# Load order, state decay on ScalarE, early attention values, and down layers with the weight units outermost

## The chip, the core and the metric

The kernel runs on one core of one Trainium2 chip. The time is that of the device, in microseconds (us), from the launch on the core to its end. Three runs of the kernel before gave 545.58, 546.04 and 546.85, so its time is the median, 546.04 us. The engines are named as in the profile: PE is TensorE, PEld its weight loads, DVE VectorE, ACT ScalarE, POOL GpSimd, and SP the engine that issues every DMA here.

## The reference

Three layers follow one another. The first is attention with a decay per head (2 sequences, 8 heads, 768 positions, 64 wide); the second multiplies two projections; the third takes the largest of three.

```python
for b in range(nb):                       # blocks of 64 positions
    intra = einsum(einsum(qb, kb) * Dmask, vb)
    inter = einsum(qb * lam_pow, kv_state)
    out[:, :, sl] = intra + inter
    kv_state = lam_block * kv_state + einsum(kb * rev_pow, vb)
x = out as (1536 tokens, 512)
x = ((x @ w_a) * (x @ w_b)) @ w_out                     # inner width 1536
y = max(max(x @ w1, x @ w2), x @ w3) @ w_out2           # inner width 768
```

q, k, v are float32; the weights are float64.

## The kernel before

**Numbers.** A weight block comes in as raw 64-bit words (`wr`, two buffers). `converted` makes float32 of it with six passes: DVE L223, ACT L226, DVE L228, ACT L231, ACT L233, DVE L235. An ACT copy (L190) then makes the high part and a DVE or POOL subtraction (L187) the low part. Every product of two float32 matrices is three matmuls: high by high, high by low, low by high. The operands x and y are split in the same way.

**Stages.** In the order of time:
- Attention works in 12 chunks n of 128 positions, the two sequences in turn. `scores(n)` is 16 matmuls (L395) into two PSUM banks, `side(n)` scales q and k on POOL (L405, L408), `masked(n)` multiplies the scores by the decay table on DVE (L418, tile `am`), and `values(n)` has up to 48 matmuls: am by v (L434), the state `stt` by q (L439) and the new state (L446). ACT then copies the result out (`x`), and DVE adds the new state to the decayed one (L458 or L460) and decays it for the chunk after the next (L463). Chunk n+2 of the same sequence needs both.
- From n = 7 on, a quarter of the first layer's plain products (L552, tile `p`) follows each chunk; then come the other groups of that layer in seven products each (L534, `zu`, `bu`, `xu`).
- `down1` (L657, tile `yp`): three tiles of 512 tokens, each of 12 units of 128 inner columns, each unit 12 matmuls over four banks. The tile is the outer loop, so each unit of the weights is wanted by the first tile 12 matmuls after the last one.
- The second layer's groups (L534, `zv`, `bv`, `xv`), whose results are folded into `m`.
- `down2` (L685, tile `out`): 12 tiles of 128 rows, each of 6 units of 3 matmuls. The weights come in four blocks of 1.5 units.

**Order.** Every engine runs its instructions in program order. A small model of the engines' times (`Pace`) sets in which order the queued tasks (conversions, splits) are written on DVE, ACT and POOL among the fixed work; `open_to` says from which point on a conversion ("conv") or its split may be written. SP issues the loads in order and waits at each until its buffer is free, so that a load of `wr` which waits for a buffer holds all later loads back. `converted` asks for the raw block two further on (L229) as soon as it has read its own.

Of the kernel before, what the change touches and what calls it, by code (L numbers as in the profile page):

```python
# [13 lines left out]
ALU = mybir.AluOpType  # L14
# [148 lines left out]
def decay_attention_gated_mlps(ctx: ExitStack, tc: tile.TileContext, qkv: bass.AP, lam: bass.AP, wup: bass.AP, wdown: bass.AP, out: bass.AP):  # L163
# [48 lines left out]
    def converted(m, width, roomy=False):  # L212
# [65 lines left out]
    def down_block(m, i):  # L278
        roomy = 2 <= i < ND1 or i == ND1 + 3
        yield "gate", ("done", m - (2 if roomy else 1))  # L280
# [12 lines left out]
        tt(e, lo[:, s], t[:, 0:WB], rd(hi[:, s]), ALU.subtract)  # L293
        pace.open(("done", m))
        for k in range(3):
            if k // 2 <= i % 2 and (i // 2, k) not in dunit and (k == 0 or i % 2):
                dunit[i // 2, k] = hi[:, 512 * k:512 * k + 512], lo[:, 512 * k:512 * k + 512]

    def items_to(m):
        while state["item"] <= min(m, len(items) - 1):  # L300
            n = state["item"]
            kind, i = items[n]
            wtask[n] = pace.opens["done", n] = pace.add((up_pair if kind == "up" else down_block)(n, i), 1 if n > 1 else -1)
            state["item"] += 1
# [72 lines left out]
    def load(n, *which):  # L377
# [4 lines left out]
        for i in which:  # L382
            of, name = ((aq, "aq"), (av, "av"))[i]
            of[n] = slot(f"{name}{n}")
            nc.sync.dma_start(out=of[n][:, 0:1024], in_=qkv[b * NC + c, i])

# [35 lines left out]
    def values(n):  # L422
# [31 lines left out]
        if c < NC - 1:  # L454
# [19 lines left out]
    class Operands:  # L474
# [5 lines left out]
        def __init__(self, a, name, order=ORDER):  # L480
# [7 lines left out]
            for i, x in enumerate(order):  # L488
                t = self.tasks[x] = pace.add(self.make(i, x, "A21" in order), 0)
                for g in ("sum", "part"):  # L490
# [140 lines left out]

    gparts, gtasks = {}, {}

    def splits_to(n):
        while len(gtasks) < min(n, NTT * K1):
            i = len(gtasks)
            t, k = divmod(i, K1)
# [3 lines left out]
            gtasks[i] = pace.add(split_part(ga[k][:, 512 * t:512 * t + 512], h, l), 0), h, l  # L641

    def down1(at):
        n = NTT * K1
        for i in range(n):
            t, k = divmod(i, K1)
            at(t, k)
            splits_to(i + 3)
            if k == 0:
                ps = [bank(f"yp{t}{e}") for e in range(KD)]  # L650
            wh, wl = unit(0, k)
            task, gh, gl = gtasks[i]
            pace.need(task)
            for e in range(KD):
                cols = slice(128 * e, 128 * e + 128)
                for m, (w, g) in enumerate(((wh, gh), (wh, gl), (wl, gh))):
                    nc.tensor.matmul(ps[e], w[:, cols], g, start=k == 0 and m == 0, stop=k == K1 - 1 and m == 2)  # L657
                pace.pe(3 * MM5)
                if k == K1 - 1:
                    o = 512 * t  # L660
                    while o < 512 * t + 512:
                        q, r = divmod(o, J)
                        m = min(J - r, 512 * t + 512 - o)
                        j, b = divmod(q, 2)
                        if (j, b) not in ya:
                            ya[j, b] = slot(f"y{j}{b}").rearrange("p (a i) -> p a i", a=KD)
                        copy(ya[j, b][:, e, r:r + m], ps[e][:, o - 512 * t:o - 512 * t + m])
                        pace.run("ACT", m)
                        o += m

    def down2(i):
        j, b, r = i // 6, i // 3 % 2, i % 3
        o = tokens(j, b).start + 128 * r
        row = b * S + j * J + 128 * r
        last = i == NT // 128 - 1
        cols = 256 if last else 512
        ob = slot(f"ob{i}")
        for c in range(0, 512, cols):
            s = slice(c, c + cols)
            ps = bank(f"out{i}_{c}")[:, s]  # L680
            for k in range(K2):
                (ah, al), (wh, wl) = hs[k], unit(ND1, k)
                pace.need(htask[k, j])
                for n, (a, w) in enumerate(((ah, wh), (al, wh), (ah, wl))):
                    nc.tensor.matmul(ps, a[:, o:o + 128], w[:, s], start=k == 0 and n == 0, stop=k == K2 - 1 and n == 2)  # L685
                pace.pe(3 * MM5 * cols / 512)
            if last and c > 0:
                nc.vector.tensor_copy(ob[:, s], ps)  # L688
            else:
                copy(ob[:, s], ps)  # L690
                pace.run("ACT", cols)
            nc.sync.dma_start(out=out[row:row + 128, s], in_=ob[:, s])

    with tc.manual_schedule():
# [8 lines left out]
        ps = bank("warm_ps")  # L703
        for i in range(9):
            nc.tensor.matmul(ps, warm[:, 0:128], warm, start=True, stop=True)
        powers()
# [7 lines left out]
        pace.t["PE"] = 6.0  # L714
        for n in range(3):
            scores(n)
        pace.t["PE"] = 12.0
        for n in range(2):
# [49 lines left out]
        for n in range(len(order)):  # L768
            load(n + 4, 0)
            load(n + 3, 1)  # L770
            if n in (1, 4):
                m = n // 4
                open_to("conv", m)
                open_to("split", m)
            if n == 7:
                open_to("conv", NPLAIN)
            if n > 0:
                scores(n + 2)
            side(n + 2)
            masked(n + 2)  # L780
            values(n)
            if n % 6 == 5:
# [57 lines left out]
        for _ in in_slots(groups, each2, finished2):  # L840
            pass
        for i in range(NT // 128):
            down2(i)

# [62 lines left out]
```

## Time and profile before

| | us |
|---|---|
| median of the three runs | 546.04 |
| the profiled execution | 545.02 |
| its span | 543.2 |
| PE busy | 511.7 (94%) |
| DVE busy | 377.4 (69%) |
| ACT busy | 280.7 (52%) |
| attention, and the quarters of the plain products in it | 0 to 72 |
| rest of the first layer | 72 to 243.5 |
| down1 | 243.5 to 346.2 |
| second layer | 346.2 to 483.3 |
| down2 | 483.3 to 540.2 |

The stages differ in what they wait for, so the shares of busy time over the whole span say little by themselves; the stretches do. The profiled execution lies 1.0 us below the median of the runs. The page's row of slices gives PE's granted clock in tenths of full speed: 9888 in the first 54 us, 7 in the slice in which down2 begins, and 9 elsewhere.

### The profile page before, as it was taken

Reading aid. Unit: us, or ns where it says so; the run is one execution under the profiler, and the core shown is the slowest. Engines: PE = TensorE matmul, PEld = TensorE weight load, DVE = VectorE, ACT = ScalarE, POOL = GpSimd, SP = SyncE. Lnnn points to the kernel's source line nnn. Section 1 sums busy time; section 2 is a strip of 40 time slices with the busy share of each in tenths; the row PEclk is TensorE's granted clock in tenths of the full one; section 3 lists DMA queues with packets and bytes.
Section 4 is the critical chain, followed back from the end, with each engine's and each line's share of the span. In section 5 each row is a group of like instructions: output and inputs, shape, how many; then the busy total and the mean of one; then the engine's idle time right before and its main releaser. Section 6 shows DMA issues by size and latency. Waiting matters only on the chain.

```text
span 543.2 us, 7761 instructions
## 1 busy us (share of the span) xinstructions
PE 511.7 (94%) x3167; PEld 469.3 (86%) x3167; DVE 377.4 (69%) x554; ACT 280.7 (52%) x419; POOL 48.2 (9%) x46
## 2 busy tenths in 40 slices
PE   4886999999999999999899999998999999978997
PEld 2765899999999999997678888798999999966886
DVE  3288888887777777489879069375898989892000
ACT  1163564765555555368887066535665566671111
POOL 1647000011111110111000000000000000000000
PEclk9888999999999999999999999999999999997999
DMA  7985310222222211015452001000222211200111
GB/s 223 406 346 209 122 74 1 78 77 78 78 78 78 77 60 58 2 59 174 151 197 78 1 0 43 36 1 0 78 78 77 80 58 59 83 34 39 59 70 66
DMA packets 11812, 48.49 MB, mean 89 GB/s; under 512 B 1272, under 2 KB 3072, under 8 KB 9088
## 3 DMA queue, kind: packets, MB, share of 16 engines
q1 hardware_dynamic: 11776, 47.99, 24.6%
q8 instruction: 25, 0.41, 0.3%
q14 instruction: 11, 0.09, 0.1%
HBM read 44.83 MB, written 3.15 MB: 88 GB/s over the span
## 4 chain that ended last, share of the span: by engine, by line
PE 77%; DVE 12%; DMA 5%; ACT 4%; issue 1%; SPq 1%; ACTq 0%
PE zu L534 15%; PE yp L657 13%; PE zv L534 11%; PE out L685 9%; PE bu L534 7%; PE p L552 7%; PE bv L534 6%; PE xu L534 4%; PE xv L534 2%; DMA aq<-qkv_dram 2%; DMA wr<-wup_dram 2%; DVE m L594 1%; PE o L434 1%; DVE wd L228 1%; DVE w L228 1%
## 5 line engine op out<-in xcount | busy, mean ns | idle before, releaser
L187 DVE TENSOR_TENSOR lo<-w,hi 128x1024 fp32r<-128x1024 f32 (+1 forms) x40 | 49.1, 1235 | 6.7 <-ACT hi L190 6.7
L190 ACT ACTIVATE hi<-w 128x1024 fp32r<-128x1024 f32 (+1 forms) x40 | 37.3, 953 | 13.3 <-DVE w L187 7.9
L657 PE MATMUL yp<-gh,dh 128*128 128x512 f32 x108 | 42.3, 391 | 1.9 <-ACT dh L190 1.9
L657 PE MATMUL yp<-gh,dl 128*128 128x512 f32 x108 | 42.2, 391 | 0.9 <-DVE dl L187 0.9
L657 PE MATMUL yp<-gl,dh 128*128 128x512 f32 x108 | 42.0, 389 | 0.0
L187 DVE TENSOR_TENSOR gl<-g,gh 128x512 fp32r<-128x512 f32 x36 | 24.7, 700 | 19.3 <-ACT gh L190 19.3
L583 POOL TENSOR_TENSOR g<-z1u,z6u 128x384 f32<-128x384 f32 x20 | 22.1, 1104 | 172.7 <-DVE z6u L565 116.6
L688 DVE COPY ob<-out 128x256 f32<-128x256 f32 x1 | 0.4, 425 | 47.6 <-PE out L685 47.6
L228 DVE SCALAR_TENSOR_TENSOR w<-wr,w 128x1024 int32<-128x1024 int32 (+1 forms) x26 | 31.1, 1196 | 0.5
L235 DVE TENSOR_TENSOR w<-w,ws 128x1024 f32<-128x1024 f32 x21 | 25.7, 1223 | 6.3 <-ACT w L233 6.2
L233 ACT ACTIVATE w<-w 128x1024 f32<-128x1024 f32 (+1 forms) x26 | 26.4, 1014 | 7.1 <-DVE w L228 6.9
L187 DVE TENSOR_TENSOR w<-w 128x256 f32<-128x256 f32 (+1 forms) x57 | 29.1, 510 | 1.2
L226 ACT ACTIVATE ws<-wr,bias 128x1024 f32<-128x1024 f32 x21 | 25.9, 1233 | 5.6 <-DMA wr<-wup_dram 5.6
L190 ACT ACTIVATE ob<-out 128x512 f32<-128x512 f32 (+1 forms) x12 | 7.0, 580 | 39.8 <-PE out L685 39.8
L657 PEld LDWEIGHTS yp<-gh,dh 128*128 128x128 f32 x108 | 20.3, 188 | 6.8 <-ACT dh L190 2.8
L190 ACT ACTIVATE z6u<-zu 128x384 f32<-128x384 f32 x20 | 9.8, 492 | 30.3 <-PE zu L534 30.3
L657 PEld LDWEIGHTS yp<-gh,dl 128*128 128x128 f32 x108 | 20.3, 188 | 6.0 <-DVE dl L187 1.8
L190 ACT ACTIVATE x<-o 128x256 f32<-128x256 f32 x24 | 8.9, 383 | 31.3 <-PE o L434 16.5
L231 ACT ACTIVATE ws<-ws,bias 128x1024 f32<-128x1024 f32 x21 | 24.1, 1148 | 0.3
L657 PEld LDWEIGHTS yp<-gl,dh 128*128 128x128 f32 x108 | 20.3, 188 | 4.1
L418 DVE TENSOR_TENSOR am<-s,tables 128x512 f32<-128x512 f32 x24 | 15.4, 682 | 10.4 <-DMA tables<-tab_d 6.4
L552 PE MATMUL p<-x0A,hi 128*128 128x384 f32 x64 | 18.4, 365 | 4.1 <-DVE x0A L187 4.1
(200 smaller groups left out, 1505.9 us busy)
## 6 DMA issues: line engine op xcount, KB each, us to landing
wr<-wup_dram SPq DMA_DIRECT2D x21, 1024.0 KB, 4.8
wr<-wdown_dram SPq DMA_DIRECT2D x12, 768.0 KB, 4.3
aq<-qkv_dram SPq DMA_DIRECT2D x12, 512.0 KB, 6.4
av<-qkv_dram SPq DMA_DIRECT2D x12, 512.0 KB, 8.5
out_dram<-ob SPq DMA_DIRECT2D x11, 256.0 KB, 2.0
tables<-tab_d SPq DMA_DIRECT2D x4, 128.0 KB, 4.0
tables<-tab_d SPq DMA_DIRECT2D x4, 64.0 KB, 4.4
out_dram<-ob SPq DMA_DIRECT2D x2, 128.0 KB, 1.7
```

The costliest lines, as they stand in the source:

```text
L187: (nc.vector if e == "DVE" else nc.gpsimd).tensor_tensor(out=o, in0=a, in1=b, op=op)
L190: nc.scalar.activation(out=o, in_=a, func=AF.Copy)
L226: nc.scalar.activation(out=sign, in_=high.bitcast(F32), func=AF.Identity, bias=bias[:, 0:1])
L228: nc.vector.scalar_tensor_tensor(out=w, in0=low, scalar=29, in1=w, op0=ALU.logical_shift_right, op1=ALU.bitwise_or)
L231: nc.scalar.activation(out=sign, in_=sign, func=AF.Sign, bias=bias[:, 1:2])
L233: nc.scalar.activation(out=f, in_=f, func=AF.Abs)
L235: nc.vector.tensor_tensor(out=f, in0=f, in1=sign, op=ALU.mult)
L534: nc.tensor.matmul(ps, w, x, start=p in FIRST and i == 0, stop=i == len(todo) - 1, skip_group_check=p not in FIRST)
L552: nc.tensor.matmul(ps, w[:, 128 * k:128 * k + 128], x[:, k], start=m == 0, stop=m == 11)
L583: nc.gpsimd.tensor_tensor(out=ga[g.n][:, tokens(g.j, 0)], in0=g.z[1], in1=g.z[6], op=ALU.mult)
L657: nc.tensor.matmul(ps[e], w[:, cols], g, start=k == 0 and m == 0, stop=k == K1 - 1 and m == 2)
L685: nc.tensor.matmul(ps, a[:, o:o + 128], w[:, s], start=k == 0 and n == 0, stop=k == K2 - 1 and n == 2)
```

## The change

It has five parts.

1. The raw weight blocks 0, 1 and 2 are loaded later (at n = 2, 7 and 9 of the attention loop), and not by the conversion of an earlier block; the loads of the last two v tiles bring only the half that is used.
2. The decay of the state (L463, one DVE instruction of 128x256) becomes four ACT instructions of 128x64.
3. Only two chunks of scores are computed ahead; `values(0)` comes before `scores(2)`, and eight more warming matmuls stand before it.
4. `down1` runs tiles 0 and 1 side by side over eight banks with the unit as the outer loop, and then tile 2. `down2` runs its first six row tiles in the same way over six banks.
5. The conversions of the last four weight blocks are opened one group later, and some tasks have other ranks.

```diff
@@ converted
-        load_to(m + 2)
+        if m > 1:
+            load_to(m + 2)
@@ values
-                nc.vector.tensor_tensor(out=stt[b], in0=std, in1=ltab[:, :, C - 1:C].to_broadcast([128, NP, 64]), op=ALU.mult)
-                pace.run("DVE", 256, kind="S")
+                for p in range(NP):
+                    nc.scalar.activation(out=stt[b][:, p], in_=std[:, p], func=AF.Copy, scale=ltab[:, p, C - 1:C])
+                    pace.run("ACT", 64)
...
+    GORDER = [(t, k) for k in range(K1) for t in range(2)] + [(2, k) for k in range(K1)]
...
     def down1(at):
+        ps = [[bank(f"yp{t}{e}") for e in range(KD)] for t in range(2)]
+        for k in range(K1):
+            for t in range(2):
+                at(t, k)
+                down1_part(t, k, ps[t])
...
+    def down2():
+        n = NT // 128
+        ps = [bank(f"out{i}") for i in range(6)]
+        for k in range(K2):
+            for i in range(6):
+                down2_part(i, k, ps[i], slice(0, 512))
+                if k == K2 - 1:
+                    store(i, 0, 512, ps[i])
+        for i in range(6, n):
...
-        for n in range(3):
+        for n in range(2):
             scores(n)
+        keep_warm(8)
...
-            if n in (1, 4):
+            if n in (2, 7):
                 m = n // 4
+                load_to(m)
                 open_to("conv", m)
                 open_to("split", m)
-            if n == 7:
+            if n == 9:
+                load_to(NPLAIN + 1)
                 open_to("conv", NPLAIN)
-            if n > 0:
-                scores(n + 2)
+            if n == 0:
+                values(n)
+            scores(n + 2)
             side(n + 2)
             masked(n + 2)
-            values(n)
+            if n > 0:
+                values(n)
...
-                for d in {N2 - 3: (0, 1), N2 - 2: (2,)}.get(n, ()):
+                for d in {N2 - 2: (0, 1), N2 - 1: (2, 3)}.get(n, ()):
                     open_to("conv", base + N2 + d)
                     open_to("split", base + N2 + d)
-            if n == N2 - 1 and g.j == 0:
-                open_to("conv", base + N2 + 3)
-                open_to("split", base + N2 + 3)
```

On SP, the loads of the attention's middle chunks before (`aq6` holds q and k of chunk 6, `av5` k and v of chunk 5, `wr0` is the first raw weight block; the number at a name's end only tells tiles apart):

```order
L385 DMA av4_212<-qkv_dram 128x1024
L206 DMA wr0_214<-wup_dram 128x1024
L385 DMA aq6_256<-qkv_dram 128x1024
L385 DMA av5_258<-qkv_dram 128x1024
L385 DMA aq7_307<-qkv_dram 128x1024
L385 DMA av6_309<-qkv_dram 128x1024
L206 DMA wr1_353<-wup_dram 128x1024
L206 DMA wr2_355<-wup_dram 128x1024
L385 DMA aq8_361<-qkv_dram 128x1024
L385 DMA av7_363<-qkv_dram 128x1024
```

And the same stretch of SP now:

```order
L387 DMA av4_223<-qkv_dram 128x1024
L387 DMA aq6_266<-qkv_dram 128x1024
L387 DMA av5_268<-qkv_dram 128x1024
L206 DMA wr0_270<-wup_dram 128x1024
L387 DMA aq7_325<-qkv_dram 128x1024
L387 DMA av6_327<-qkv_dram 128x1024
L387 DMA aq8_382<-qkv_dram 128x1024
L387 DMA av7_384<-qkv_dram 128x1024
L387 DMA aq9_436<-qkv_dram 128x1024
L387 DMA av8_438<-qkv_dram 128x1024
```

The first weight block moved behind two attention loads, and the second and third (`wr1`, `wr2`), at which SP waited for a free buffer, moved out of this stretch: `wr1` now stands behind the loads of chunk 11's q and of the half of chunk 10's v, and `wr2` behind the last of all, that of chunk 11's v.

On DVE, the first conversion among the attention's work before (`w0` is the first float32 block, `am4` the masked scores of chunk 4, `o2_1` an output bank of chunk 2):

```order
L418 TENSOR_TENSOR am3_228<-s3_0_216,tables_79 128x512
L418 TENSOR_TENSOR am3_228<-s3_1_217,tables_79 128x512
L223 TENSOR_SCALAR w0_249<-wr0_214 128x1024
L458 COPY stt_81<-o1_1_232 128x256
L463 TENSOR_TENSOR stt_81<-stt_81,tables_79 128x256
L418 TENSOR_TENSOR am4_272<-s4_0_260,tables_79 128x512
L418 TENSOR_TENSOR am4_272<-s4_1_261,tables_79 128x512
L460 TENSOR_TENSOR stt_81<-o2_1_276,stt_81 128x256
L463 TENSOR_TENSOR stt_81<-stt_81,tables_79 128x256
L418 TENSOR_TENSOR am5_323<-s5_0_311,tables_79 128x512
L418 TENSOR_TENSOR am5_323<-s5_1_312,tables_79 128x512
L228 SCALAR_TENSOR_TENSOR w0_249<-wr0_214,w0_249 128x1024
```

And now:

```order
L460 COPY stt_81<-o1_1_241 128x256
L223 TENSOR_SCALAR w0_282<-wr0_270 128x1024
L420 TENSOR_TENSOR am4_288<-s4_0_272,tables_79 128x512
L420 TENSOR_TENSOR am4_288<-s4_1_273,tables_79 128x512
L228 SCALAR_TENSOR_TENSOR w0_282<-wr0_270,w0_282 128x1024
L462 TENSOR_TENSOR stt_81<-o2_1_292,stt_81 128x256
L420 TENSOR_TENSOR am5_342<-s5_0_329,tables_79 128x512
L420 TENSOR_TENSOR am5_342<-s5_1_330,tables_79 128x512
L236 TENSOR_TENSOR w0_282<-w0_282,ws0_284 128x1024
L462 TENSOR_TENSOR stt_81<-o3_1_346,stt_81 128x256
L420 TENSOR_TENSOR am6_399<-s6_0_386,tables_79 128x512
L420 TENSOR_TENSOR am6_399<-s6_1_387,tables_79 128x512
```

The conversion's first pass stands ahead of the masked scores of chunk 4 in both; its second and third moved up by two chunks; the decay (L463) is gone from DVE.

On PE, the start of down2 before (`dh`, `dl`, the two parts of a weight unit, `hh`, `hl` those of the activations):

```order
L685 MATMUL out0_0_4308<-dh8_4157,hh0_3421 128x512
L685 MATMUL out0_0_4308<-dh8_4157,hl0_3422 128x512
L685 MATMUL out0_0_4308<-dl8_4158,hh0_3421 128x512
L685 MATMUL out0_0_4308<-dh8_4157,hh1_3837 128x512
L685 MATMUL out0_0_4308<-dh8_4157,hl1_3838 128x512
L685 MATMUL out0_0_4308<-dl8_4158,hh1_3837 128x512
```

And now:

```order
L700 MATMUL out0_4325<-dh8_4247,hh0_3453 128x512
L700 MATMUL out0_4325<-dh8_4247,hl0_3454 128x512
L700 MATMUL out0_4325<-dl8_4248,hh0_3453 128x512
L700 MATMUL out1_4326<-dh8_4247,hh0_3453 128x512
L700 MATMUL out1_4326<-dh8_4247,hl0_3454 128x512
L700 MATMUL out1_4326<-dl8_4248,hh0_3453 128x512
```

After three matmuls of a row tile the next unit followed (`hh1`); now the next row tile (`out1`) follows with the same unit, and the second unit comes 18 matmuls after the first. In down1 the second tile likewise follows each unit's 12 matmuls, so that the next unit comes after 24.

## Rows read from the trace of the kernel before

**Rows 1.** Windows: length, busy us and instructions of each engine, clock, DMA share, GB/s.

```profile
0.00:72.00 72.00, 56.31 (x762) 45.30 (x763) 47.97 (x82) 26.51 (x44) 26.12 (x26) 0.93 0.70 260
...
243.50:275.00 31.50, 28.30 (x120) 21.76 (x119) 27.87 (x37) 25.37 (x35) 1.67 (x1) 1.00 0.53 182
275.00:346.20 71.20, 71.20 (x315) 58.97 (x315) 42.95 (x58) 39.15 (x67) 0.00 (x0) 1.00 0.14 49
```

**Rows 2.** Waits of PE: line, what it waited for, total us, times, longest us.

```profile
PE s L395 <- DMA aq<-qkv_dram: 7.0, 4, 4.9
PE p L552 <- DVE x0A L187: 4.1, 1, 4.1
...
PE o L434 <- DVE stt L458: 2.3, 1, 2.3
PE yp L657 <- ACT dh L190: 1.9, 2, 1.1
...
PE yp L657 <- DVE dl L187: 0.9, 2, 0.4
```

**Rows 3.** Chain that ends last, 0 to 100 us: start us, us, what.

```profile
15.86 10.89 DMA wr<-wup_dram
...
28.26 1.20 DVE am L418 x2
...
51.11 3.92 PE p L552 x11
...
58.36 2.29 PE p L552 x12
...
71.79 25.16 PE p L552 x144
```

**Rows 4.** Timeline of SP: start us, us, what it issues.

```profile
21.81 11.53 SPq L206 DMA_DIRECT2D wr<-wup_dram  x2
```

**Rows 5.** Window of 10 us, columns as in rows 1.

```profile
20.00:30.00 10.00, 7.73 (x131) 6.44 (x130) 3.81 (x9) 2.55 (x5) 6.91 (x7) 0.88 1.02 419
```

**Rows 6.** Timeline of DVE in attention: start us, us, what, idle before it.

```profile
26.77 0.69 DVE L223 TENSOR_SCALAR w<-wr 128x1024 int32<-128x1024 int32 x1 [6.12 <-DMA wr<-wup_dram]
...
49.05 3.96 DVE L187 TENSOR_TENSOR x0A<-x,x0A 128x768 fp32r<-128x768 f32 x2
...
54.79 0.95 DVE L187 TENSOR_TENSOR x0A<-x,x0A 128x768 fp32r<-128x768 f32 x1
```

**Rows 7.** Groups of DVE instructions by line: busy us, mean ns, idle before.

```profile
L463 DVE TENSOR_TENSOR stt<-stt,tables 128x256 f32<-128x256 f32 x8 | 5.2, 653 | 0.3
```

**Rows 8.** Groups of ACT instructions by line, columns as in rows 7.

```profile
L226 ACT ACTIVATE ws<-wr,bias 128x1024 f32<-128x1024 f32 x21 | 25.9, 1233 | 5.6 <-DMA wr<-wup_dram 5.6
L231 ACT ACTIVATE ws<-ws,bias 128x1024 f32<-128x1024 f32 x21 | 24.1, 1148 | 0.3
...
L233 ACT ACTIVATE w<-w 128x1024 f32<-128x1024 f32 x21 | 22.1, 1054 | 4.7 <-DVE w L228 4.6
...
L190 ACT ACTIVATE x<-o 128x256 f32<-128x256 f32 x24 | 8.9, 383 | 31.3 <-PE o L434 16.5 <-PE o L439 11.7 <-PE o L446 2.9
...
L190 ACT ACTIVATE y<-yp 128x128 f32<-128x128 f32 x8 | 2.2, 275 | 6.7 <-PE yp L657 6.6
```

**Rows 9.** Timeline of POOL in attention, columns as in rows 6.

```profile
48.80 3.39 POOL L405 TENSOR_TENSOR aq<-aq,tables 128x512 f32<-128x512 f32 x2
```

**Rows 10.** Timeline of PE in down1, at its start.

```profile
243.56 0.39 PE L657 MATMUL yp<-gh,hd 128*128 128x512 f32 x1
```

**Rows 11.** Timeline of PE in down2, its start and two stops.

```profile
483.31 0.40 PE L685 MATMUL out<-dh,hh 128*128 128x512 f32 x1
...
487.41 0.50 PE L685 MATMUL out<-dh,hl 128*128 128x512 f32 x1 [2.31 <-DVE hl L187]
...
491.76 0.79 PE L685 MATMUL out<-hd,hh 128*128 128x512 f32 x1 [2.66 <-ACT hd L190]
```

**Rows 12.** Chain that ends last, 480 to 543.2 us, columns as in rows 3.

```profile
491.76 48.48 PE out L685 x222
```

More of the change, by code (lines that the diff above doesn't have):

```diff
@@ L384, in load @@
             of[n] = slot(f"{name}{n}")
[L385 removed]
+            s = slice(512 if i == 1 and c == NC - 1 else 0, 1024)
+            nc.sync.dma_start(out=of[n][:, s], in_=qkv[b * NC + c, i, :, s])
     def scores(n):
@@ L488, in __init__ @@
             for i, x in enumerate(order):
-                t = self.tasks[x] = pace.add(self.make(i, x, "A21" in order), 0)
+                t = self.tasks[x] = pace.add(self.make(i, x, "A21" in order), 0.7 if "A21" in order and x[0] == "S" else 0)
                 for g in ("sum", "part"):
@@ L640, in splits_to @@
             h, l = (x[:, 512 * (k % 3):512 * (k % 3) + 512] for x in gparts[t, k // 3])
-            gtasks[i] = pace.add(split_part(ga[k][:, 512 * t:512 * t + 512], h, l), 0), h, l
-    def down1(at):
[L644 to L669, printed above, removed]
@@ L671, in down2, with down1_part @@
-    def down2(i):
+            gtasks[t, k] = pace.add(split_part(ga[k][:, 512 * t:512 * t + 512], h, l), 0), h, l
+    def down1_part(t, k, ps):
+        splits_to(GORDER.index((t, k)) + 4)
+        wh, wl = unit(0, k)
+        task, gh, gl = gtasks[t, k]
+        pace.need(task)
+        for e in range(KD):
+            cols = slice(128 * e, 128 * e + 128)
+            for m, (w, g) in enumerate(((wh, gh), (wh, gl), (wl, gh))):
+                nc.tensor.matmul(ps[e], w[:, cols], g, start=k == 0 and m == 0, stop=k == K1 - 1 and m == 2)
+            pace.pe(3 * MM5)
+            if k == K1 - 1:
+                o = 512 * t
+                while o < 512 * t + 512:
+                    q, r = divmod(o, J)
+                    m = min(J - r, 512 * t + 512 - o)
+                    j, b = divmod(q, 2)
+                    if (j, b) not in ya:
+                        ya[j, b] = slot(f"y{j}{b}").rearrange("p (a i) -> p a i", a=KD)
+                    copy(ya[j, b][:, e, r:r + m], ps[e][:, o - 512 * t:o - 512 * t + m])
+                    pace.run("ACT", m)
+                    o += m
@@ L672, in down2, with store @@
+    def down1(at):
+        ps = [[bank(f"yp{t}{e}") for e in range(KD)] for t in range(2)]
[3 more added lines that the diff above has]
+                down1_part(t, k, ps[t])
+        ps = [bank(f"yp2{e}") for e in range(KD)]
+        for k in range(K1):
+            at(2, k)
+            down1_part(2, k, ps)
+    def store(i, c, cols, ps, vector=False):
         j, b, r = i // 6, i // 3 % 2, i % 3
-        o = tokens(j, b).start + 128 * r
         row = b * S + j * J + 128 * r
-        last = i == NT // 128 - 1
@@ L676, in down2 @@
[L676 to L692, printed above, removed]
+        s = slice(c, c + cols)
@@ new lines, in store, with down2_part @@
+        if c == 0:
+            store.ob = slot(f"ob{i}")
+        ob = store.ob
+        if vector:
+            nc.vector.tensor_copy(ob[:, s], ps)
+        else:
+            copy(ob[:, s], ps)
+            pace.run("ACT", cols)
+        nc.sync.dma_start(out=out[row:row + 128, s], in_=ob[:, s])
+    def down2_part(i, k, ps, s):
+        o = tokens(i // 6, i // 3 % 2).start + 128 * (i % 3)
+        (ah, al), (wh, wl) = hs[k], unit(ND1, k)
+        pace.need(htask[k, i // 6])
+        for n, (a, w) in enumerate(((ah, wh), (al, wh), (ah, wl))):
+            nc.tensor.matmul(ps, a[:, o:o + 128], w[:, s], start=k == 0 and n == 0, stop=k == K2 - 1 and n == 2)
+        pace.pe(3 * MM5 * (s.stop - s.start) / 512)
@@ new lines, in down2 @@
+    def down2():
[7 more added lines that the diff above has]
+        for i in range(6, n):
+            last = i == n - 1
+            cols = 256 if last else 512
+            for c in range(0, 512, cols):
+                p = bank(f"out{i}_{c}")[:, c:c + cols]
+                for k in range(K2):
+                    down2_part(i, k, p, slice(c, c + cols))
+                store(i, c, cols, p, last and c > 0)
@@ L703, in decay_attention_gated_mlps, with keep_warm @@
         ps = bank("warm_ps")
-        for i in range(9):
-            nc.tensor.matmul(ps, warm[:, 0:128], warm, start=True, stop=True)
+        def keep_warm(n):
+            for i in range(n):
+                nc.tensor.matmul(ps, warm[:, 0:128], warm, start=True, stop=True)
+        keep_warm(9)
         powers()
@@ L841, in decay_attention_gated_mlps @@
             pass
-        for i in range(NT // 128):
-            down2(i)
+        down2()
 def kernel(**inputs):
```

11 lines of the change are left out of this document (5 added, 6 removed).

## The prediction

> **What bounds the kernel now.** I read the stretches by stage first, then the waits of PE, then the chain of work that ends last, and for each wait the timelines of the engines around it. The stretches show where PE stands still: it is busy for 56.3 of the first 72 us, for 28.3 of the 31.5 us in which down1 begins, and without a gap in the rest of down1 [rows 1]. So the whole program is bound by PE except in three places, and a gain in DVE's or ACT's work counts only there.
>
> Place one is attention. PE's largest waits are there: 7.0 us for q tiles, 4.1 for the first split of x, 2.3 for a state [rows 2]. The chain names one cause for most of it: the transfer of wr0 from 15.86 to 26.75, on which DVE sits for 6.12 us with its first conversion pass [rows 3, 6], and then SP, which stands for 11.53 us at wr1 and wr2 while the q and v loads queue behind it [rows 4]. At 51.11 PE starts the first quarter of plain products, 4.1 us late, and runs it at half clock (3.92 us, against 2.29 for the next one); 16.76 us after that quarter's end, at 71.79, attention is over [rows 3].
>
> Place two is the start of down1. A matmul of 128x512 costs 71.20 / 315 = 0.2260 us where nothing is late [rows 1]. Its 432 matmuls (3 tiles by 12 units by 12) are worth 97.6 us; the stage takes 102.6, from 243.56 to 346.2 [rows 10, 1]. The 5.0 us between are five stops for weight parts, of which dh and dl make 2.8 [rows 2], and the refill after each.
>
> Place three is the start of down2: 216 full matmuls, 48.8 us, but it takes from 483.31 to 540.24, 56.9 [rows 11, 12]. The 8.1 us between are the stops that end at 487.41 (for hl) and 491.76 (for the third weight block's high part) [rows 11], the half clock that follows the second (0.79 for a matmul that took 0.40), and refills.
>
> **The change, part by part.** Attention first. wr0 now stands behind two attention loads of 0.52 MB. At the 419 GB/s at which the queue runs there [rows 5] that is 2 × 1.25 = 2.5 us, so wr0 lands at W = 26.75 + 2.5 = 29.25. DVE still has wr0's first pass ahead of the masked scores of chunk 4, so DVE's wait is not gone; it grows, and PE runs dry once more, until about W + 1.8 (the pass 0.69, the two masked halves 1.20 [rows 6, 3], at pipelined steps). What goes is SP's 11.53 us: no load of attention waits for a raw buffer any more. From W on the engines' own chain is the limit, in program order:
> - values(4) needs the state of chunk 2, whose decay stands on ACT behind wr0's sign pass: 1.23 for that pass, 0.7 for two x copies, DVE's sum 0.4, the decay 0.9, then PE's 1.2 of matmuls: W + 5.4 with the steps of queueing, an estimate, = 34.65. Before, the same point came at 34.67 in the trace, so nothing is gained up to here, and the early values bring nothing either.
> - values(5) needs the state of chunk 3, which DVE adds only after its last pass over wr0, and that waits for ACT's two other passes (1.15 and 1.05 [rows 8]): W + 9.9.
> - values(6) has the split of wr0 ahead of it on DVE (ACT's high part 1.06, DVE's low part 1.23): W + 13.4. values(7) is a PE chunk of 3.33 us (58.36 − 55.03 [rows 3]) later: W + 16.7. The first quarter, at full clock, takes 2.29: W + 19.0 = 48.25, against 55.03.
>
> That is 6.8 us earlier. It needs DVE and POOL not to disturb each other. Where two DVE subtractions met two POOL multiplications they took 3.96, against 2 × 0.95 alone, and POOL 3.39 [rows 6, 9]; one such meeting costs the chain 1.8 to 2.0, so the other bound is 5.0. I take 5.9. After the quarter the order is the one of before, so the rest of attention keeps its 16.76, and the first layer behind it was bound by PE and shifts as a block.
>
> By the Trainium skill ("SBUF — State Buffer", section "SBUF: two separate sides") a DVE operation with two SBUF inputs and a GpSimd operation take the shared port pair as an exclusive lock and the loser blocks; with POOL now free to run ahead on loads that come earlier, that rule points to the 5.0 end. The rows agree in the sum (1.9 of DVE and the POOL work in about 4 us).
>
> The decay itself: on DVE it cost 0.653 in the mean, eight times [rows 7]. On ACT no 128x64 row exists; a copy of 128x128 takes 0.275 and of 128x256 0.383 [rows 8], which puts 128x64 at 0.22 on that line, so four cost 0.9; the bounds are 4 × 0.275 = 1.1 above and 0.653, as if nothing changed, below. On the chain it stands in chunks 2 to 5 only, so it adds 4 × (0.9 − 0.65) = 1.0 us there (0 to 1.8), already in the W terms; DVE is freed of 5.2 us beside it, which is what lets the x splits come in time. ACT has room: 26.5 busy of 72 [rows 1], and 8 × 0.9 = 7.2 more fits.
>
> The Trainium skill ("ScalarE: Activation LUTs", section "Rules for kernel authors") speaks against this edit: it says to multiply on VectorE, not ScalarE. By that rule alone the edit would lose on every chunk of the chain; rows 7 and 8 bear out the sign per instruction, and the sum would be 0.8 us worse at the upper bound.
>
> The smaller last v loads and eight warming matmuls lie beside work that waits for q anyway (7.0 us [rows 2]), and cost nothing; without that cover the eight would cost 8 × 0.4, the length of a full-clock 128x512 matmul [rows 10], 3.2 us.
>
> Down1: two tiles side by side make a unit of weights last 24 matmuls, 5.42 us, instead of 12, 2.71. DVE's need per unit is about 2.1 to 2.3 for the weights (four passes over 128x768 at about 0.95 less steps [rows 6], per 1.5 units) and 0.65 per split of g, so before 2.9 against 2.71 (late), now 3.6 against 5.42 (early). (0.65 is 0.95 × 512 / 768, an estimate.) A weight part that came just too late for unit k is wanted k × 2.71 us later than before, counted from the stage's start. All five stops go, and in the third tile, which runs alone, every weight is there. I take −4.8, with 3 and 5.0 as bounds: the lower leaves two stops of 0.9 to 1.1.
>
> Down2: a unit now lasts 18 matmuls, 4.07 us. hl of the second unit came 487.41 − 483.31 = 4.1 after the stage's start and is needed 4.07 after it: just in time, at worst tenths late. The third block's high part came 8.45 after it, and its units, the fourth and the fifth, are needed 16.3 and 20.3 after it. The stops go, with them the idle stretch ahead of the half clock. The conversions were opened one group later, which takes DVE work out of the second layer's end and puts it behind its last products: that may delay the operands by one block's passes, 4 × 0.95 = 3.8 us, and the fourth unit has 7.8 to spare. I take −7.9; bounds 4 (half the stops come back at unit 1) and 8.1. The tail behind the last matmul stays.
>
> The sum against the profiled 545.02: −5.9 − 4.8 − 7.9 = −18.6, 526.4. The median lies 1.0 above the profiled execution, so the forecast is 527.4.
>
> **The rivals.**
> - Attention gives nothing: wr0's later landing, POOL in DVE's way, and a low clock after the longer idle eat SP's 11.53. For it: the point at 34.65 is no earlier, and DVE's wait for wr0 stays [rows 6]. Against it: the q waits behind SP come after that point [rows 4]. 545.02 − 12.7 + 1.0 = 533.3.
> - The lower layers keep some of their stops, because the later conversions land behind DVE's other work and unit 1 of down2 has no margin: 4 us come back, 531.4.
> - Attention is not held by wr0's conversion but by PE alone after W. Then four chunks of 3.33 and the quarter follow W + 1.8: W + 17.4 at most, 1.6 better; and if wr0 lands as before, 2.5 more. 523.3, and with down1 and down2 at their upper bounds 522.9.
> - The change does not do what it says in its early values: they wait for q of chunk 3 as before. I hold this for true, and it is in the forecast at zero.
> - Slower: PE falls to half clock in the two idle stretches (before chunk 3's scores, and before W + 1.8) and stays there to attention's end. Eight chunks of 3.33 and four quarters of 2.29 are 35.8 us of full-clock work, and would take twice that: 526.4 + 35.8 + 1.0 = 563.2. It outweighs the gain once more than 18.6 us of that work, about half, run at the low clock. For it: the quarter of 3.92 after a stop of 4.1 [rows 2, 3]. Against it: the very next quarter took 2.29, and the whole first 72 us had 0.93 of the clock [rows 1].
>
> **How the numbers follow.** The forecast has a chance of 0.63 (524.5 to 530 by its own bounds), attention without gain 0.13, the lower layers' stops 0.11, the better attention 0.08, slower 0.03, and 0.02 that the parts cancel to nothing. The range takes in both middle rivals and the better one: 521.5 to 534. Two runs of this kernel are told apart from about 0.2% (1.1 us) on; faster by more than that has 0.95, within it 0.02, slower 0.03.
>
> **What would show it.** SP without a stop over 2 us before 55 us; wr0 landing at 29 to 30; the first p matmul after the one-off at 45 to 48 instead of 51.1, at 0.18 us each rather than 0.36; attention over at 65 to 67. Down1 without a stop, 97.6 to 98.5 us from its first matmul to its last, and down2 49 to 50. The prediction is wrong if the p quarter starts at 50 or later, if PE's clock in the first 66 us is below 0.9, or if down2 still has a stop of over 1 us.

## The result, and the profile after

The changed kernel takes 528.32 us (median of four runs, 528.27 to 528.49) against 546.44 for the kernel before, run beside it: a ratio of 0.967, 95% interval 0.9653 to 0.9687. The forecast was 527.4 in 521.5 to 534. The profiled execution after has 528.49 us and a span of 526.7; before it was 545.02 and 543.2. So the two profiles differ by 16.5 us and the medians by 18.1: the kernel before lies 1.4 below its median in its profile, the one after 0.2 above. One execution among the later experiments (the profiled one of no_side) ran at a granted clock of 0.656 from end to end and is used for nothing but VectorE's times.

The difference of 16.5 by stage, each from the start of its first matmul (attention from the start of the span) to the start of the next stage's first:

| stage | before | after | difference | forecast |
|---|---|---|---|---|
| attention with its quarters | 71.72 | 67.35 | −4.4 | −5.9 |
| rest of the first layer | 171.84 | 171.72 | −0.1 | 0 |
| down1 | 102.67 | 97.96 | −4.7 | −4.8 |
| second layer | 137.08 | 137.25 | +0.2 | 0 |
| down2, to the end of its last matmul | 56.9 | 49.4 | −7.5 | −7.9 |

SP's timeline after answers to [rows 4] and to the first of [rows 3]: start, us, what it issues.

```profile
17.18 0.33 SPq L206 DMA_DIRECT2D wr<-wup_dram  x1
...
37.12 0.42 SPq L206 DMA_DIRECT2D wr<-wup_dram  x1
...
40.89 56.36 SPq L206 DMA_DIRECT2D wr<-wup_dram  x4
```

wr0 is issued behind two more attention loads, and no load of attention stands behind a wait for a raw buffer any more: the wait of 56.36 us at the end is for blocks that come after the last v tile. The chain after, in the stretch of [rows 3] (a piece of PE in it begins where the one before it ends, up to 0.2 us behind the matmul's own start in the table):

```profile
17.18 12.19 DMA wr<-wup_dram
29.39 0.70 DVE w L223
30.09 1.19 DVE am L420 x2
...
48.15 2.51 PE p L555 x12
...
53.99 2.29 PE p L555 x12
...
67.42 25.16 PE p L555 x144
```

wr0 landed at 29.39 (forecast 29.25). The first plain quarter starts at 48.15, runs at full clock (2.51 us against 3.92 before) and attention ends at 67.42, the 67.35 of the table. The waits of PE, answering to [rows 2]:

```profile
PE s L397 <- DVE am L420: 3.5, 1, 3.5
...
PE o L436 <- DVE am L420: 2.1, 2, 1.1
PE bv L537 <- DVE lo L187: 1.7, 1, 1.7
PE s L397 <- DMA aq<-qkv_dram: 1.5, 2, 0.9
PE zv L537 <- ACT z6v L190: 1.3, 1, 1.3
```

The waits for q fell from 7.0 to 1.5, and all waits of `yp` and `out` are gone, and so is the 4.1 for x. New are 2.1 of the early values for their masked scores, and one wait of 3.5: scores of chunk 6 need the bank of the masked scores of chunk 4, which stand on VectorE behind the first pass over wr0. (Of the later passes, the second moved up by one chunk, from behind the masked scores of chunk 5 to behind those of chunk 4, and only the third by two.) The timelines of PE, DVE and POOL, in that order, show it and what follows (the last two answer to [rows 6, 9]):

```profile
30.74 2.33 PE L397 MATMUL s<-aq 64*128 64x128 f32 x16 [3.50 <-DVE am L420]
33.01 1.97 PE L436 MATMUL o<-am,av 128*64 128x128 f32 x16
```

```profile
29.39 0.70 DVE L223 TENSOR_SCALAR w<-wr 128x1024 int32<-128x1024 int32 x1 [8.64 <-DMA wr<-wup_dram]
...
35.87 2.03 DVE L236 TENSOR_TENSOR w<-w,ws 128x1024 f32<-128x1024 f32 x1 [1.92 <-ACT w L234]
...
40.31 1.85 DVE L187 TENSOR_TENSOR lo<-w,hi 128x1024 fp32r<-128x1024 f32 x1 [0.88 <-ACT hi L190]
...
46.45 0.96 DVE L187 TENSOR_TENSOR x0A<-x,x0A 128x768 fp32r<-128x768 f32 x1 [1.86 <-ACT x0A L190]
```

```profile
36.93 1.88 POOL L410 TENSOR_TENSOR av<-av,tables 128x512 f32<-128x512 f32 x1
...
41.03 3.49 POOL L407 TENSOR_TENSOR aq<-aq,tables 128x512 f32<-128x512 f32 x2
```

After the stop the 16 score matmuls take 2.33 and not 1.16: PE runs at 1.2 GHz from there to 36.0 (granted clock 0.50 from 30.7 on), some 5 us. The two passes over w0 that meet POOL's multiplications take 2.03 and 1.85, and 1.23 elsewhere. In the lower layers the chain of the span's second half has one piece for each:

```profile
239.23 97.96 PE yp L654 x432
...
474.45 49.25 PE out L700 x234
```

432 matmuls of down1 in 97.96 us are 0.2268 each, and the 234 of down2 (216 full ones' worth) are 49.25: neither stage has a stop left.

### The profile page after: what moved, and what is told of

It reads as the page before. It is cut to its first block, busy times and chain, and to the rows that moved or that the text cites. A ratio compares the mean times of both kernels' runs of the same rounds, so it can differ in the third digit from the quotient of the medians.

```text
span 526.7 us, 7797 instructions
## 1 busy us (share of the span) xinstructions
PE 508.4 (97%) x3175; PEld 469.2 (89%) x3175; DVE 364.1 (69%) x546; ACT 284.8 (54%) x451; POOL 50.5 (10%) x46
## 3 DMA queue, kind: packets, MB, share of 16 engines
HBM read 44.30 MB, written 3.15 MB: 90 GB/s over the span
## 4 chain that ended last, share of the span: by engine, by line
PE 86%; DVE 5%; DMA 4%; ACT 2%; issue 1%; SPq 1%; ACTq 0%; DVEq 0%
PE yp L654 19%; PE zu L537 16%; PE zv L537 13%; PE out L700 9%; PE bu L537 8%; PE p L555 7%; PE bv L537 7%; PE xu L537 4%; PE xv L537 3%; DMA wr<-wup_dram 2%; DMA aq<-qkv_dram 1%; PE o L436 1%; DVE m L597 1%; ACT stt L466 1%; DVE lo L187 1%
## 5 line engine op out<-in xcount | busy, mean ns | idle before, releaser
L187 DVE TENSOR_TENSOR lo<-w,hi 128x1024 fp32r<-128x1024 f32 (+1 forms) x40 | 44.1, 1109 | 11.8 <-ACT hi L190 11.8
L586 POOL TENSOR_TENSOR g<-z1u,z6u 128x384 f32<-128x384 f32 x20 | 25.1, 1258 | 172.8 <-DVE z6u L568 155.4
L187 DVE TENSOR_TENSOR gl<-g,gh 128x512 fp32r<-128x512 f32 x36 | 25.8, 725 | 13.3 <-ACT gh L190 13.3
L190 ACT ACTIVATE z7u<-zu 128x384 f32<-128x384 f32 x20 | 9.8, 491 | 35.5 <-PE zu L537 35.4
L654 PEld LDWEIGHTS yp<-gh,dl 128*128 128x128 f32 x108 | 20.3, 188 | 4.2
L654 PEld LDWEIGHTS yp<-gl,dh 128*128 128x128 f32 x108 | 20.3, 188 | 4.2
L654 PEld LDWEIGHTS yp<-gh,dh 128*128 128x128 f32 x108 | 20.3, 188 | 4.1
L223 DVE TENSOR_SCALAR w<-wr 128x1024 int32<-128x1024 int32 (+1 forms) x26 | 17.5, 674 | 8.7 <-DMA wr<-wup_dram 8.6
L190 ACT ACTIVATE ob<-out 128x512 f32<-128x512 f32 (+1 forms) x12 | 7.0, 580 | 29.2 <-PE out L700 28.8
L568 DVE TENSOR_TENSOR z7u<-bu,z7u 128x384 f32<-128x384 f32 x20 | 11.1, 556 | 15.4 <-ACT z7u L190 15.4
L190 ACT ACTIVATE gh<-g 128x512 fp32r<-128x512 f32 x36 | 21.5, 618 | 0.0
```

What stands on the lines that cost most here:

```text
L187: (nc.vector if e == "DVE" else nc.gpsimd).tensor_tensor(out=o, in0=a, in1=b, op=op)
L190: nc.scalar.activation(out=o, in_=a, func=AF.Copy)
L586: nc.gpsimd.tensor_tensor(out=ga[g.n][:, tokens(g.j, 0)], in0=g.z[1], in1=g.z[6], op=ALU.mult)
```

## The experiments

Each is timed against the kernel before, run beside it on one chip. There are three such groups: loads_only, decay_dve, no_early and conv_at3 (546.00 before); no_side, conv3_rank, down1_tiles and down2_tiles (547.14); the other four (547.25). Kernels of different groups are best compared by their ratios. The stages are lengths, read from each one's own profile as in the table above; "attention" runs from the start of the span to the start of the plain products that follow its last chunk.

| kernel | median | ratio, 95% interval | attention | to down1 | down1 | second layer | down2 |
|---|---|---|---|---|---|---|---|
| loads_only | 543.36 | 0.9947 (0.9927 to 0.9967) | 68.50 | 171.82 | 102.73 | 137.11 | 56.95 |
| down_only | 533.64 | 0.9752 (0.9730 to 0.9774) | 73.56 | 172.06 | 97.96 | 137.27 | 49.40 |
| decay_dve | 531.11 | 0.9730 (0.9708 to 0.9751) | 69.66 | 172.07 | 97.96 | 137.23 | 49.39 |
| no_early | 528.88 | 0.9680 (0.9657 to 0.9704) | 67.47 | 171.73 | 97.96 | 137.23 | 49.39 |
| no_warm | 528.72 | 0.9663 (0.9643 to 0.9683) | 67.01 | 171.72 | 97.96 | 137.21 | 49.40 |
| down1_tiles | 533.65 | 0.9747 (0.9724 to 0.9770) | 67.94 | 171.72 | 102.71 | 137.23 | 49.39 |
| down2_tiles | 539.65 | 0.9863 (0.9837 to 0.9888) | 67.75 | 171.73 | 97.96 | 138.78 | 60.60 |
| no_side | 530.35 | 0.9685 (0.9659 to 0.9710) | – | – | – | – | – |
| no_side_again | 531.35 | 0.9705 (0.9679 to 0.9731) | 65.63 | 174.29 | 97.96 | 137.24 | 49.40 |
| conv_at3 | 529.10 | 0.9683 (0.9662 to 0.9704) | 63.57 | 174.50 | 97.96 | 138.80 | 49.39 |
| conv3_rank | 525.39 | 0.9601 (0.9575 to 0.9626) | 63.72 | 171.73 | 97.96 | 137.26 | 49.39 |
| after_again | 528.77 | 0.9673 (0.9648 to 0.9698) | 67.62 | 171.73 | 97.96 | 138.81 | 49.39 |

**The load order alone (loads_only).** Part 1 of the change on the kernel before, cut to its main lines. The loads and the opening of the first three conversions move together, so that the conversions too are opened later here (n = 2, 7 and 9 for 1, 4 and 7).

```diff
-        load_to(m + 2)
+        if m > 1:
+            load_to(m + 2)
...
-            if n in (1, 4):
+            if n in (2, 7):
                 m = n // 4
+                load_to(m)
```

> The kernel before with the new order of loads alone (no decay on ScalarE, no early values, the lower layers as before). Theory (SP's stand of 11.53 us at wr1 and wr2 held attention back): the load order carries all of attention's gain, which was 4.4 us (71.79 to 67.42), so about 542.0 against 546.4, attention over at 66.5 to 68.5. Rival (the decay on ScalarE and the early values make the room on DVE that the load order needs): attention over at 70 to 72, 545 to 546.5.

Attention ended at 68.50: 3.2 of the 4.4 us, nearer the theory; in the medians it is 2.6 (546.00 to 543.36). The rival has part of the truth: the first quarter still started late and at half clock (3.89 us), since PE waited 5.1 for x0A, and VectorE has no gap from 29.2 to 51.4. That its later opening of the conversions did nothing here is not shown.

**The lower layers alone (down_only).** The change with its attention parts undone; the ranks stay changed.

> The kernel before with the new order of down1 and down2, the later opening of the last conversions and the ranks, attention as before. Theory (the three places are independent): down1 97.9 to 98.1 and down2 49.4 to 49.6, 546.0 less 4.7 less 7.5 = 533.8, within 0.7. Rival (the lower layers' stops depend on what attention leaves behind on VectorE): 536 to 540.

Both stages are as long as in the full change, to 0.01 us, so they don't depend on attention; 533.64 is the theory's number. Attention itself came out 1.8 later than before. Down to the first split of x, VectorE's instructions stand in the order of before, so the ranks don't show in it yet; what differs is PE's stop for a q tile, here first before and then in down_only:

```profile
39.52 1.16 PE L395 MATMUL s<-aq 64*128 64x128 f32 x16 [1.52 <-DMA aq<-qkv_dram]
```

```profile
40.50 2.08 PE L395 MATMUL s<-aq 64*128 64x128 f32 x16 [3.86 <-DMA aq<-qkv_dram]
```

The tile came 1.0 later and half clock followed, there and again behind the first quarter (1.76 for 16 scores). The profiled execution is also 1.4 above this kernel's median (535.05 against 533.64). So the 1.8 may belong to this one execution; that the ranks cost anything is not shown.

**The decay back on VectorE (decay_dve).**

```diff
-                for p in range(NP):
-                    nc.scalar.activation(out=stt[b][:, p], in_=std[:, p], func=AF.Copy, scale=ltab[:, p, C - 1:C])
+                nc.vector.tensor_tensor(out=stt[b], in0=std, in1=ltab[:, :, C - 1:C].to_broadcast([128, NP, 64]), op=ALU.mult)
```

> The changed kernel with the decay of the state back on VectorE. Theory (the decay stands on the chain from wr0 to the first plain quarter and four ScalarE instructions cost 1.06 us against 0.42 to 0.83 for one of VectorE): attention ends 0.5 to 2 us earlier, 526.5 to 528.0. Rival (VectorE is what limits this stretch and the 5.2 us taken from it are the gain): attention ends 2 to 4 us later, 530 to 532.

2.8 us slower (531.11 against 528.32; the intervals of the two ratios lie apart): my theory fell, and the rival holds, with nearly its number. VectorE's timeline in this kernel:

```profile
35.20 0.87 DVE L465 TENSOR_TENSOR stt<-stt,tables 128x256 f32<-128x256 f32 x1
...
37.19 2.12 DVE L236 TENSOR_TENSOR w<-w,ws 128x1024 f32<-128x1024 f32 x1
...
39.68 1.06 DVE L465 TENSOR_TENSOR stt<-stt,tables 128x256 f32<-128x256 f32 x1
...
42.30 0.88 DVE L465 TENSOR_TENSOR stt<-stt,tables 128x256 f32<-128x256 f32 x1
...
44.30 1.21 DVE L187 TENSOR_TENSOR lo<-w,hi 128x1024 fp32r<-128x1024 f32 x1
...
45.88 0.43 DVE L465 TENSOR_TENSOR stt<-stt,tables 128x256 f32<-128x256 f32 x1
...
48.21 3.56 DVE L187 TENSOR_TENSOR x0A<-x,x0A 128x768 fp32r<-128x768 f32 x4
```

Its whole timeline has no gap from 29.4 to 52 us. With POOL beside it a decay takes 0.83 to 1.06, not the 0.43 of the next ones alone, so the six between wr0 and the splits of x are 4.5 us of the engine that the whole stretch waits for; the low part of w0 is made at 44.30 (40.31 in the changed kernel) and the splits of x at 48.21 (46.45). Of the 2.3 us of attention, 1.1 are the quarter's later start (49.21 for 48.15); the rest is half clock after PE's stop of 3.7 for x, 0.4 in the quarter and 0.8 in the scores behind it (1.92 on the chain for 1.09). The four ScalarE instructions on the other side:

```profile
L466 ACT ACTIVATE stt<-stt,tables 128x64 f32<-128x64 f32 x32 | 8.5, 336 | 8.1 <-DVE stt L462 7.1 <-DVE stt L460 1.0
```

Each takes 0.336 by itself; the timeline has a set of four at 1.06, near the upper bound of 1.1 and not the 0.9 that I took. ScalarE has the room for it.

**No early values (no_early), no extra warming (no_warm).** In the one three chunks of scores go ahead again, values follow the next scores, and the extra warming is out too; the other only drops `keep_warm(8)`.

> The changed kernel with three chunks of scores ahead again, values after the next scores from the first chunk on, and without the eight additional warming matmuls. Theory (early values bring nothing, since the landing of q of chunk 3 at 17 to 18 us sets the next step in both): 528.3 within 0.5. Rival (they bring the first state and the bank for the later scores forward): 529.5 to 531.

> The changed kernel without the eight additional warming matmuls ahead of the first values. Theory (they lie beside the wait for the first decay tables): within 0.5 of after_again. Rival (they hold TensorE's clock up for the first values): the first values run at half clock for longer, but the next q lands at 17 to 18 us whatever they do, so attention ends no more than 0.5 later; a third outcome, over 1 us slower, would show that the early values do work after all.

Both are the changed kernel to within 0.6 us of attention and 0.6 us of the median. The early values bring nothing, as forecast. What differs in attention is the landing of wr0 (29.52 and 29.04): the first quarter starts 18.75 after it in both, as in the changed kernel.

**Conversion of block 0 later (conv_at3).**

```diff
             if n in (2, 7):
                 m = n // 4
                 load_to(m)
+            if n in (3, 7):
+                m = n // 4 if n == 7 else 0
                 open_to("conv", m)
                 open_to("split", m)
```

> The changed kernel with the conversion of weight block 0 opened one chunk later (at n = 3 in place of 2), the load at the same place; the first pass over wr0 then stands behind the masked scores of chunk 4 and the state of chunk 2 on VectorE. Theory (VectorE's wait for wr0 holds the masked scores of chunk 4 and so PE for 3.5 us before scores of chunk 6): that stop goes, the first plain quarter starts at 45 to 47 in place of 48.15, 525.5 to 527.5. Rival (the six passes of the conversion after wr0's landing set the quarter, whatever stands ahead of them): 528.3 within 0.5, and a stop of the same size further on.

Half of each: the stop shrank from 3.5 to 1.0, the quarter started at 44.37 and attention ended 3.8 earlier, which is the theory, but the time did not move. PE's timeline where 2.8 of it were given back (idle before, and releaser, in brackets):

```profile
102.81 0.62 PE L537 MATMUL zu<-x0A,hi 128*128 128x384 f32 x2 [1.52 <-ACT hi L190]
104.07 0.44 PE L537 MATMUL zu<-x0A,lo 128*128 128x384 f32 x1 [0.64 <-DVE lo L187]
```

That is the first use of block 3, whose conversion kept its place on VectorE and ScalarE while PE came 3.8 us earlier. The other 1.6 went in the second layer, by the clock (last section).

**Block 3 ahead as well (conv3_rank).** On top of conv_at3:

```diff
-{0: -1, 2: 0.5}.get(n, 1)
+{0: -1, 2: 0.5, 3: 0.6}.get(n, 1)
```

> The changed kernel with the conversion of block 0 opened at n = 3 and a rank of 0.6 for block 3, so that its conversion stands ahead of the last splits of x on VectorE and ScalarE. Theory (with block 0 later, 3.8 us were gained in attention and 2.8 given back at the first use of block 3, whose conversion kept its place behind the splits of x): attention over at 63.5 to 64, no stop over 1 us before down1, 524.5 to 526.5. Rival (VectorE has too much work between 63 and 104 us, in whatever order): a stop of 2 to 3 us at another operand there, 527.5 to 529.5.

Attention over at 63.72, the first layer behind it in 171.73, no stop there: 525.39, 0.9601 (0.9575 to 0.9626), below the changed kernel's interval both times that it was measured (0.9653 to 0.9687, and after_again). It is the best version here.

**POOL beside VectorE (no_side, no_side_again).** POOL's multiplications of chunks 6 to 11 are left out.

> The changed kernel with POOL's two multiplications left out for chunks 6 to 11 (values then read the unscaled q and k of those chunks, so that part of the computation is left out); the order on the other engines is the same. Theory (POOL beside VectorE stretches two passes of wr0's conversion, 2.03 and 1.85 us in place of 1.23, and they stand on the chain to the first plain quarter): both passes take 1.2 to 1.25, the quarter starts 1.2 to 1.6 us earlier than 48.15, 526.7 to 527.2. Rival (the half clock of TensorE after its stop at 30.74 sets the quarter): the passes get shorter and the quarter stays at 47.8 to 48.3, 528.1 to 528.5.

> The same kernel as no_side (POOL's two multiplications left out for chunks 6 to 11, so that part of the computation is left out), whose one profiled execution had a granted clock of 0.656 from end to end and shows nothing of TensorE's times. There the two passes of wr0's conversion took 1.23 each, as the theory has it, but the median of the other runs, 530.35 beside 547.14 for the kernel before, was no better than the changed kernel's ratio. Theory as before: the quarter starts at 46.5 to 47.0 and the gain of 1.4 is given back behind attention. Rival: TensorE's half clock sets the quarter, which starts at 47.8 to 48.3, and the time is that of the changed kernel run beside it.

VectorE and then PE in no_side_again:

```profile
35.55 1.23 DVE L236 TENSOR_TENSOR w<-w,ws 128x1024 f32<-128x1024 f32 x1 [1.92 <-ACT w L234]
...
39.18 1.23 DVE L187 TENSOR_TENSOR lo<-w,hi 128x1024 fp32r<-128x1024 f32 x1 [0.88 <-ACT hi L190]
```

```profile
46.41 0.58 PE L557 MATMUL p<-x0A,hi 128*128 128x384 f32 x2 [0.19 <-DVE am L420]
...
105.70 0.44 PE L539 MATMUL zu<-x0A,lo 128*128 128x384 f32 x1 [1.32 <-DVE lo L187]
```

Both passes take 1.23, which is 0.80 and 0.62 less than in the changed kernel, and the quarter starts 17.34 after wr0's landing (29.07), not 18.76 (29.39 to 48.15): 1.42 earlier, the sum of the two. PE has its stop and the slow scores behind it here too (1.94 for 16), though for a shorter time than in the changed kernel's profile. After_again, with POOL at work, tells the two apart; its wr0 landing, its quarter, and the stretch behind the stop (length, busy times, granted clock third from the end), with that of the changed kernel's first profile last:

```profile
29.67 0.69 DVE L223 TENSOR_SCALAR w<-wr 128x1024 int32<-128x1024 int32 x1 [7.28 <-DMA wr<-wup_dram]
```

```profile
48.42 0.58 PE L555 MATMUL p<-x0A,hi 128*128 128x384 f32 x2 [0.19 <-DVE am L420]
```

```profile
30.70:36.00 5.30, 4.98 (x62) 4.25 (x64) 3.53 (x6) 3.75 (x9) 3.76 (x4) 0.68 1.03 420
```

```profile
30.70:36.00 5.30, 5.26 (x50) 4.38 (x50) 3.38 (x6) 3.74 (x9) 4.11 (x4) 0.50 1.02 419
```

With the clock at 0.68 or at 0.50, the quarter starts 18.75 or 18.76 after the landing. So the contention, and not the clock, held the quarter. The gain is given back at the same place as in conv_at3 (1.32 for block 3's low part; the first layer is 2.6 longer). The times fit neither forecast: no_side took 530.35, where 526.7 to 528.5 were expected, and no_side_again 531.35, 2.6 above after_again, though its profiled execution has a span 1.0 shorter. No profile of the slower executions exists, and why they are slower stays open.

**The order in down1 and down2 undone, one at a time (down1_tiles, down2_tiles).** The tile is the outer loop again (in down1 with the splits of g three ahead and not four); all else is the changed kernel.

> The changed kernel with down1 in the order of before: the tile as the outer loop, four banks, the splits of g three ahead. Theory (the place of a unit's next use is what removed the stops): down1 takes 102 to 103 us again in place of 97.96, 532.5 to 533.5. Rival (the other ranks and the gate of the second down block made the weights early enough): down1 at 98 to 100, 528.3 to 530.5.

> The changed kernel with down2 in the order of before (all six units of a row tile, then the next tile), the conversions opened one group later kept. Theory (the order of units alone hides the last conversions): down2 takes 57 to 60 us in place of 49.4, since the conversions come no earlier than before, 536 to 539. Rival (opening the conversions later is itself the gain, by freeing VectorE for the last groups' results): down2 at 50 to 54, 529 to 533.

PE's stops in the two, first down1_tiles, then down2_tiles:

```profile
258.06 0.50 PE L654 MATMUL yp<-gh,dh 128*128 128x512 f32 x1 [1.13 <-ACT dh L190]
...
259.24 0.50 PE L654 MATMUL yp<-gh,dl 128*128 128x512 f32 x1 [0.45 <-DVE dl L187]
...
268.06 0.50 PE L654 MATMUL yp<-gh,dh 128*128 128x512 f32 x1 [0.82 <-ACT dh L190]
...
269.24 0.50 PE L654 MATMUL yp<-gh,dl 128*128 128x512 f32 x1 [0.45 <-DVE dl L187]
```

```profile
477.41 0.49 PE L700 MATMUL out<-dh,hh 128*128 128x512 f32 x1 [0.33 <-ACT dh L190]
...
479.79 0.50 PE L700 MATMUL out<-dl,hh 128*128 128x512 f32 x1 [1.65 <-DVE dl L187]
...
484.34 0.80 PE L700 MATMUL out<-hd,hh 128*128 128x512 f32 x1 [3.35 <-ACT hd L190]
...
487.77 0.80 PE L700 MATMUL out<-hd,hh 128*128 128x512 f32 x1 [1.64 <-ACT hd L190]
```

down1_tiles has the stops of before, to a few hundredths ([rows 2] has 1.9 and 0.9 for the same two pairs), and 4.75 us. In down2 the old order with the later conversions is worse than before (60.6 against 56.9); with the units outermost they cost nothing. No kernel with the new down2 and the conversions opened as before was run, so whether they had to move is left open.

**The change again (after_again).** 

> The changed kernel itself, on the chip of the others: the ratio of 0.967 to the kernel before again, and the quarter at 48.15. Every theory expects the same; it is the measure for the three others.

It gave 0.9673, the quarter at 48.42 and attention at 67.62; wr0 landed 0.3 later, which accounts for both.

## Why the prediction was right, point by point

- **wr0 at 29.25.** 29.39, and 29.0 to 30.0 in the other profiles with this load order. The sum of two loads at the rate of [rows 5] holds.
- **SP's 11.53 go, attention gains 5.0 to 6.8, 5.9 taken.** It gained 4.4, under the lower bound: the meetings with POOL and the decay were sized too small. Without POOL in the way the quarter was to start at W + 16.7 and end at W + 19.0; it started at W + 18.8 and ended at W + 21.3 (50.66). Of the 2.3 between, 1.4 are the two meetings of VectorE with POOL; I had taken half of one meeting at 1.8 to 2.0. 0.6 remain with POOL idle (17.34 in no_side_again), which three or four decays of 1.06 in place of 0.9 would fill, an estimate; 0.2 are the quarter itself. That PE fell to half clock in its stop was left out of the working, and it moved values(4) to W + 7.3 in place of 5.4, but after_again and no_side_again show that the quarter didn't wait for it.
- **The decay costs 1.0 on the chain.** The wrong sign. 0.9 was 1.06, but the whole edit gained 2.3 us of attention: the 0.653 of [rows 7] is a mean of instructions alone and beside POOL, and with the decay on it VectorE, not the chain through ScalarE, is the engine without a gap. I had counted the 5.2 us freed only as something that "lets the x splits come in time", with no price. The load order alone gave 3.2 and the decay 2.3, more than the 4.4 together; what takes the 1.1 back was not tried apart. The rule of the Trainium skill ("ScalarE: Activation LUTs", section "Rules for kernel authors") to multiply on VectorE and not on ScalarE is borne out for one multiplication (0.42 alone on VectorE against 1.06), but not for this stretch, where VectorE becomes the bound.
- **The lock of VectorE and GpSimd.** The Trainium skill ("SBUF — State Buffer", section "SBUF: two separate sides") has the two block each other, which pointed to the 5.0 end, and the runs agree: a pass of 1.23 takes 2.03 and 1.85 beside POOL, and 1.23 with POOL idle.
- **Early values and warming at zero.** no_early and no_warm bear it out.
- **Down1 −4.8.** −4.7, and down1_tiles brings the same stops back.
- **Down2 −7.9.** −7.5: 49.4 where 216 full matmuls at 0.2268 are 49.0. The "just in time" of the working is misread. Before, seven matmuls stand ahead of the stop for hl at 487.41 [rows 11], three to a unit; the first ones of the second and the third unit are:

```profile
484.02 0.39 PE L685 MATMUL out<-dh,hh 128*128 128x512 f32 x1
...
484.71 0.39 PE L685 MATMUL out<-dh,hh 128*128 128x512 f32 x1
```

So that hl is the third unit's, wanted 8.1 and not 4.07 after the stage's start in the new order: it had 4 us of room. The block of the other stop is the last of the four, and the 16.3 and 20.3 are right for its units, the fifth and the sixth. For the later conversions (room of 7.8 us) the 60.6 of down2_tiles shows what they cost without that room: 3.7 over the 56.9 of before, though that kernel has other ranks too. In the changed kernel the third block had the least room, its low part ready at 484.08 for a matmul at 487.03:

```profile
483.12 0.96 DVE L187 TENSOR_TENSOR ld<-w,hd 128x768 fp32r<-128x768 f32 x1
```

```profile
487.03 0.39 PE L700 MATMUL out<-ld,hh 128*128 128x512 f32 x1
```

- **The median 1.0 above the profile.** In profiles the terms gave −16.5, not −18.6; in medians −18.1. The two errors, 2.1 too much gain and an offset of 1.0 that turned out −0.2, cancel in part; that the forecast came within 0.9 of the median is luck to that extent. Why the kernel before lies 1.4 below its median in its profile stays open. Its granted clock is 0.984 there and 0.972 to 0.981 in nearly all its other executions, and the one after has 0.990 to 0.994 in all; but another execution of the kernel before took the same 545.02 at 0.978, so the clock alone doesn't tell.
- **The signs.** wr0's landing, down1 and down2 came as said, and none of the three signs of a wrong prediction appeared (quarter at 48.15, clock 0.92 in the first 66 us, no stop in down2). Two came just outside: the quarter (48.15 for 45 to 48) and attention's end (67.35 for 65 to 67). "SP without a stop over 2 us before 55 us" did not come true: SP stood 6.3 us for a free q buffer until 36.16, and at the weight blocks from 40.89 on. Neither held a load of attention behind a raw buffer.

## What to carry to other kernels

Weigh an instruction moved between engines by the engine that has no gap in that stretch, and at its duration beside its neighbour, not by the mean of the instruction. Where a stage starves at its start, let each operand serve more tiles before the next is needed (here two tiles or six side by side), which hides a conversion at no cost in work. A stop taken away early only pays if the next operands in line move too: two experiments gained 1.7 and 3.8 us in attention and lost 2.6 and 2.8 at block 3, and for one of them a rank gave it back.

## What the runs showed of the hardware

The same stop does not always lead to the low clock. The second layer has a stop of 1.7 us at the same matmul in every version. In the profile of the changed kernel and of after_again, which are the same program, the stretch behind it reads (length, busy times, the granted clock as third figure from the end):

```profile
369.00:375.00 6.00, 5.99 (x34) 6.00 (x35) 5.33 (x8) 1.55 (x2) 0.00 (x0) 1.00 0.51 172
```

```profile
369.40:375.00 5.60, 5.60 (x24) 5.60 (x25) 3.50 (x5) 1.55 (x2) 0.00 (x0) 0.70 0.49 158
```

At 0.70 that stretch costs 1.6 us (138.81 against 137.25 for the stage). conv_at3 and down2_tiles show the same 1.6. So in these profiles part of the spread between executions of one program is which of its stops are followed by 1.2 GHz.
